# A gated FFT-and-SSM layer with its gradients: a serial copy between the phases is moved, one of two PSUM copies changes engine, PSUM names and table sets are re-planned, and the tail is rebuilt

## The chip, the cores and the metric

The kernel runs on one core of a Trainium2 chip. The metric is the device time of one execution in microseconds (us), less is better. Engines are named as in the profile: PE is TensorE, PEld its weight loads, DVE is VectorE, ACT is ScalarE, POOL is GpSimd, SP is SyncE (used here only to issue DMAs). A name with q (SPq, ACTq) is the engine's instruction queue.

## The reference

```
g  = sigmoid((x * gate_w).sum(-1))                       # x: 2048 x 1024 bf16
a  = irfft2(rfft2(x) * (w_r + i w_i))                    # spectral filter, over both axes
K  = Re sum_n C[d,n] exp(dt[d] A[d,n] l) dt[d] B[d,n]    # S4 kernel, n = 0..127, l = 0..2047
b  = causal_conv(x, K) + x * Dskip                       # by FFT of length 4096
out = g * a + (1 - g) * b
```

The kernel returns `out` (out_0) and, for a given grad_out, the gradients with respect to all twelve inputs: x (out_1), w_r and w_i (out_2, out_3, 2048 x 513 bf16 each), A, B and C real and imaginary (out_4 to out_9, 1024 x 128 bf16 each), log_dt, Dskip and gate_w (out_10 to out_12).

## The kernel before, in words

All Fourier transforms are written as matrix products with tables of sines and cosines. The work has four stages, in this order.

**Phase A**, the two-dimensional spectral filter, is run twice: `run_pass(False)` for the value, `run_pass(True)` for the gradient. The second pass leaves the gradients of w_r and w_i in two DRAM scratch tensors, wgr_scr and wgi_scr, whose rows are padded from 513 to 544 columns. After it stands a barrier over all engines.

**The seam.** The padded rows are copied to out_2 and out_3 through one SBUF tile, wt, of a pool with one buffer: load, store, load, store, all on the GpSimd queue (L569, L570). The pool is closed after that, and the pools of the next stage use its memory: their first loads (PB_c and PB_s, the transform tables, 2 MB each, L592 and L593) wait for it. Some smaller constants follow, and another barrier.

**Phase B**, the state-space convolution, works through eight blocks `bi` of 128 channels. A block loads its columns of x and grad_out (L787, L788), multiplies grad_out by 1 - g (xg_blk, L790), makes tables of powers on ACT and DVE (Exp and Sin, L791 to L831), transforms forward (`FWD`), multiplies the spectra (`CMUL`) and transforms back (`INV`) into GK_blk. Then comes the part that the change touches most, here called the state-space part: 16 sub-blocks of 8 channels, in four groups `tg` of four. For each group:

- `bcast_rows` (L848 to L857) fetches two rows of a small table to SBUF (bc_rows, on the GpSimd queue) and spreads them over 128 partitions by two matmuls into PSUM: into pE and pF for the exponents, into pG and pH for the phases.
- Four pairs of exponentials on ACT make EAg for the whole group (L865, L866).
- Then, for each sub-block: Ts is scaled out of pG and pH on ACT (L874, L875); DVE takes it modulo one turn (FsFc, L880, and again a quarter turn on, L882 and L883); ACT takes the sine twice (L881, L884); DVE multiplies by EAg into AtJ and AtR (L885, L886). In two halves of four channels, TensorE transposes AtJ into pD (L895) and AtR into pC (L898), DVE copies both into the SBUF tile Ad (L900, L901), and TensorE multiplies Ad into psK (L907, L908) and AtJ and AtR into psT (L913). psK and psT lie in pA and pB for even sub-blocks and in pE and pF for odd ones. DVE copies psK out to KT_blk (L914), ACT copies psT out to Tsb (L916).
- After the four sub-blocks, ten DVE operations reduce Tsb to res4 (L923 to L934), which goes to the DRAM scratch res_scr (L936).

Exp and Sin need different function tables on ACT, so a group has two table loads (ACT_TABLE_LOAD, put down to L866 and L881). At the end of the block a last `FWD`, two `CMUL` and an `INV` make this block's output and gradient.

**The tail.** After a last barrier a loop over 16 row tiles adds the gate's part to the gradient of x (gxc, o1c) and multiplies x into gate_w's gradient; the pool fin has two buffers. Then the parameter gradients are loaded, `load_T` transposes the four B and C matrices, `cplx` and single operations compute the rest elementwise on DVE, and, when all six are ready, 48 tiles of 128x128 are transposed, copied (otile) and stored, all on the SP queue.

The order on each engine is that of the program text, moved only by a scheduler that places each instruction by its dependences; semaphores between engines follow from the tiles that an instruction reads and writes.

Of the kernel before, what the change touches and what calls it, by code (L numbers as in the profile page):

```python
# [10 lines left out]
dt = mybir.dt  # L11
ACT = mybir.ActivationFunctionType
ALU = mybir.AluOpType
# [6 lines left out]
def kernel(  # L20
# [10 lines left out]
    nc = tc.nc  # L31
    P = 128
# [5 lines left out]
    SH = S // 2  # L38
# [24 lines left out]

    pid_i = cpool.tile([P, 1], dt.int32, name="pid_i")
# [9 lines left out]
    nc.vector.memset(pio2_b[:], math.pi / 2)  # L74
    zero_b = cpool.tile([P, 1], dt.float32, name="zero_b")
# [124 lines left out]


    if CFG["phaseA"]:
        with ExitStack() as actx:
# [358 lines left out]
            RB = 32  # L562
            NPW = S // RB
            with tc.tile_pool(name="wgout", bufs=1) as wgo:
                for (scr_t, dst) in ((wgr_scr, out_2), (wgi_scr, out_3)):
                    for p0 in range(0, NPW, P):
                        npp = min(P, NPW - p0)
                        wt = wgo.tile([npp, RB, WCOL], dt.bfloat16, name="wt")
                        nc.gpsimd.dma_start(out=wt[:, :, :], in_=scr_t[p0 * RB:(p0 + npp) * RB, 0:WCOL].rearrange("(q r) c -> q r c", r=RB))  # L569
                        nc.gpsimd.dma_start(out=dst[p0 * RB:(p0 + npp) * RB, :].rearrange("(q r) c -> q r c", r=RB), in_=wt[:, :, :])  # L570

    if CFG["phaseB"]:
# [13 lines left out]
        with ExitStack() as bctx:  # L586
# [3 lines left out]
            PB_c = bconst.tile([P, MC, SH + 1], dt.bfloat16, name="PB_c")  # L590
            PB_s = bconst.tile([P, MC, SH + 1], dt.bfloat16, name="PB_s")
# [172 lines left out]
            for bi in range(NBLK):  # L764
# [25 lines left out]
                nc.vector.tensor_tensor(out=xg_blk[:, :, :, DBS:2 * DBS], in0=go_blk[:], in1=omg_bc, op=ALU.mult)  # L790
# [56 lines left out]
                with tc.tile_pool(name="ssm", bufs=1, side="right") as ssmp, tc.tile_pool(name="ssm2", bufs=2, side="right") as ssm2, \  # L847
                        tc.tile_pool(name="bm", bufs=1, side="right") as bm:  # L848
                    def bcast_rows(scr2, dg0, tagA, tagB):
                        rows = ssm2.tile([2, Ds * N], dt.bfloat16, name="bc_rows")  # L850
                        nc.gpsimd.dma_start(out=rows[:, :], in_=scr2[:, dg0:dg0 + Ds, :].rearrange("a d n -> a (d n)"))  # L851
                        HNF = Ds * N // 2
                        ps0 = psB.tile([P, HNF], dt.float32, name=tagA)
                        ps1 = psB.tile([P, HNF], dt.float32, name=tagB)
                        for hh, pst in enumerate((ps0, ps1)):
                            nc.tensor.matmul(pst[:, :], lhsT=ones_row[:, :], rhs=rows[:, hh * HNF:(hh + 1) * HNF], start=True, stop=True)  # L856
                        return ps0, ps1  # L857
                    HNF = Ds * N // 2
                    for tg in range(NTG):
                        Tsb = bm.tile([P, DG, 4, C16], dt.bfloat16, name="Tsb", bufs=2)  # L860
                        EAg = bm.tile([P, TG, Ds * N], dt.bfloat16, name="EAg", bufs=2)
                        for sbl in range(TG):
                            dg0 = d0 + (tg * TG + sbl) * Ds
                            pz0, pz1 = bcast_rows(zr2_scr, dg0, "pE", "pF")
                            nc.scalar.activation(out=EAg[:, sbl, 0:HNF], in_=pz0[:, :], func=ACT.Exp, scale=twop[:, 0:1])  # L865
                            nc.scalar.activation(out=EAg[:, sbl, HNF:2 * HNF], in_=pz1[:, :], func=ACT.Exp, scale=twop[:, 0:1])  # L866
                        for sbl in range(TG):
# [13 lines left out]
                            nc.scalar.activation(out=scv[:, 0, :], in_=FsFc[:, 0, :], func=ACT.Sin, scale=-TWO_PI / (2 ** KFA), bias=pi_b[:])  # L881
                            nc.vector.tensor_single_scalar(out=Ts[:], in_=Ts[:], scalar=(2 ** KFA) // 4, op=ALU.add)  # L882
                            nc.vector.tensor_single_scalar(out=FsFc[:, 1, :], in_=Ts[:], scalar=(2 ** KFA) - 1, op=ALU.bitwise_and)  # L883
                            nc.scalar.activation(out=scv[:, 1, :], in_=FsFc[:, 1, :], func=ACT.Sin, scale=-TWO_PI / (2 ** KFA), bias=pi_b[:])  # L884
                            nc.vector.tensor_tensor(out=AtJ[:], in0=EAg[:, sbl, :], in1=scv[:, 0, :], op=ALU.mult)  # L885
                            nc.vector.tensor_tensor(out=AtR[:], in0=EAg[:, sbl, :], in1=scv[:, 1, :], op=ALU.mult)  # L886
                            psK = psB.tile([P, Ds * C16], dt.float32, name=("pA" if sbl % 2 == 0 else "pE"))
                            psT = psB.tile([P, Ds * 4 * C16], dt.float32, name=("pB" if sbl % 2 == 0 else "pF"))
                            NQ = 4
                            for q in range(Ds // NQ):  # L890
# [10 lines left out]
                                nc.vector.tensor_copy(out=Ad[:, 0, :, :], in_=ptrR[:, :, :])  # L901
# [81 lines left out]

            tc.strict_bb_all_engine_barrier()
            fin = bctx.enter_context(tc.tile_pool(name="fin", bufs=2))
            nc.vector.tensor_reduce(out=gg[:].rearrange("p a b -> p (a b)"), in_=ggall[:].rearrange("p n a b -> p (a b) n"), axis=AX.X, op=ALU.add)
            grad_s = bconst.tile([P, 2, MC], dt.float32, name="grad_s")
# [30 lines left out]
            with tc.tile_pool(name="pg", bufs=1) as pg:  # L1018
                gwr_t = pg.tile([P, D], dt.float32, name="gwr_t")
                gwi_t = pg.tile([P, D], dt.float32, name="gwi_t")  # L1020
                Hr_t = pg.tile([P, D], dt.float32, name="Hr_t")
                Hi_t = pg.tile([P, D], dt.float32, name="Hi_t")
                nc.sync.dma_start(out=gwr_t[:], in_=res_scr[0, :, :])
                nc.sync.dma_start(out=gwi_t[:], in_=res_scr[1, :, :])
                nc.scalar.dma_start(out=Hr_t[:], in_=res_scr[2, :, :])
                nc.scalar.dma_start(out=Hi_t[:], in_=res_scr[3, :, :])
                dt_b = pg.tile([P, D], dt.float32, name="dt_b")
                nc.gpsimd.dma_start(out=dt_b[:], in_=B_log_dt.partition_broadcast(P))
                nc.scalar.activation(out=dt_b[:], in_=dt_b[:], func=ACT.Exp)
                BrT = pg.tile([P, D], dt.bfloat16, name="BrT")  # L1030
                BiT = pg.tile([P, D], dt.bfloat16, name="BiT")
                CrT = pg.tile([P, D], dt.bfloat16, name="CrT")
                CiT = pg.tile([P, D], dt.bfloat16, name="CiT")
                load_T(BrT, B_B_re, 0)
                load_T(BiT, B_B_im, 1)
                load_T(CrT, B_C_re, 0)
                load_T(CiT, B_C_im, 1)
                dBr = pg.tile([P, D], dt.float32, name="dBr2")
                dBi = pg.tile([P, D], dt.float32, name="dBi2")
                nc.vector.tensor_tensor(out=dBr[:], in0=dt_b[:], in1=BrT[:], op=ALU.mult)  # L1040
                nc.vector.tensor_tensor(out=dBi[:], in0=dt_b[:], in1=BiT[:], op=ALU.mult)
                wi_t = pg.tile([P, D], dt.float32, name="wi_t")
                nc.vector.tensor_scalar(out=wi_t[:], in0=wJ[:], scalar1=-1.0, scalar2=None, op0=ALU.mult)
# [10 lines left out]
                gCr = pg.tile([P, D], dt.float32, name="gCr")  # L1054
                gCi = pg.tile([P, D], dt.float32, name="gCi")
                cplx(gCr[:], gCi[:], gwr_t[:], gwi_t[:], dBr[:], dBi[:], True)
                gdBr = pg.tile([P, D], dt.float32, name="gdBr")
                gdBi = pg.tile([P, D], dt.float32, name="gdBi")
                cplx(gdBr[:], gdBi[:], gwr_t[:], gwi_t[:], CrT[:], CiT[:], True)
                gzr = pg.tile([P, D], dt.float32, name="gzr")  # L1060
                gzi = pg.tile([P, D], dt.float32, name="gzi")
                cplx(gzr[:], gzi[:], Hr_t[:], Hi_t[:], wR[:], wi_t[:], True)
                gBr = pg.tile([P, D], dt.float32, name="gBr")
                gBi = pg.tile([P, D], dt.float32, name="gBi")
                nc.vector.tensor_tensor(out=gBr[:], in0=gdBr[:], in1=dt_b[:], op=ALU.mult)
                nc.vector.tensor_tensor(out=gBi[:], in0=gdBi[:], in1=dt_b[:], op=ALU.mult)
                gAr = pg.tile([P, D], dt.float32, name="gAr")
                gAi = pg.tile([P, D], dt.float32, name="gAi")
                nc.vector.tensor_tensor(out=gAr[:], in0=gzr[:], in1=dt_b[:], op=ALU.mult)
                nc.vector.tensor_tensor(out=gAi[:], in0=gzi[:], in1=dt_b[:], op=ALU.mult)  # L1070
                gdp = pg.tile([P, D], dt.float32, name="gdp")
                nc.vector.tensor_tensor(out=gdp[:], in0=gdBr[:], in1=BrT[:], op=ALU.mult)
                nc.vector.tensor_tensor(out=ta[:], in0=gdBi[:], in1=BiT[:], op=ALU.mult)
                nc.vector.tensor_tensor(out=gdp[:], in0=gdp[:], in1=ta[:], op=ALU.add)
                nc.vector.tensor_tensor(out=ta[:], in0=gzr[:], in1=ArT[:], op=ALU.mult)
                nc.vector.tensor_tensor(out=gdp[:], in0=gdp[:], in1=ta[:], op=ALU.add)
                nc.vector.tensor_tensor(out=ta[:], in0=gzi[:], in1=AiT[:], op=ALU.mult)
                nc.vector.tensor_tensor(out=gdp[:], in0=gdp[:], in1=ta[:], op=ALU.add)
                gl = pg.tile([1, D], dt.float32, name="gl")
# [7 lines left out]
                for oi, (src_t, dst) in enumerate(((gAr, out_4), (gAi, out_5), (gBr, out_6), (gBi, out_7), (gCr, out_8), (gCi, out_9))):  # L1087
                    for dc in range(DC):
                        ptq = psB.tile([P, P], dt.float32, name=PSN[(oi * DC + dc) % 4])
                        nc.tensor.transpose(ptq[:, :], src_t[:, dc * P:(dc + 1) * P], ident_f[:, :])  # L1090
                        otile = fin.tile([P, P], dt.bfloat16, name="otile")
# [35 lines left out]
```

## Time and profile before

The median of six runs is 3777.74 us (3773.22 to 3783.92); the profiled execution spans 3775.0 us.

| stage | from, to (us) | length |
|---|---|---|
| phase A | 0 to 882 | 882 |
| seam: copies through wt | 882 to 939 | 57 |
| constants, barrier | 939 to 961 | 22 |
| eight blocks | 961 to 3630 | 2669 |
| of these, the state-space part of block 0 | 1056 to 1212 | 156 |
| tail | 3630 to 3775 | 145 |

In a profile row, `L901 DVE COPY Ad<-pC ... x256 | 108.5, 424 | 87.4 <-PE pC L898 83.2` reads: line 901, a copy on DVE from pC to Ad, 256 times, 108.5 us busy in all and 424 ns each; before them DVE stood idle for 87.4 us, of which 83.2 ended with PE's write of pC at line 898. A row of a table by windows has the stretch, its length, the busy time of PE, PEld, DVE, ACT and POOL with the number of instructions, the granted TensorE clock, the busy share of the DMA engines, and GB/s.

### The profile page before, as it was taken

The numbers are of one execution on the slowest core, as the hardware profiler recorded it, in microseconds if no ns is written. First come the engines' busy times: TensorE is split into PE (matmuls) and PEld (weight loads), VectorE is DVE, ScalarE is ACT, GpSimd is POOL, SyncE is SP. The second block draws the span as 40 slices with busy tenths as digits, with TensorE's granted clock in tenths as the row PEclk, the third lists the DMA queues.
The fourth block names the chain that finished last, engine by engine and source line by source line (L and its number), as shares of the span: only waits on it lengthen the run. The fifth ranks groups of instructions, "written<-read, shape, count | busy, mean of one in ns | idle before, by whom it ended". The sixth has DMA issues, their size and how long they took to land.

```text
span 3775.0 us, 56588 instructions
## 1 busy us (share of the span) xinstructions
PE 2514.2 (67%) x22305; PEld 1594.6 (42%) x22388; DVE 2586.9 (69%) x5624; ACT 1309.9 (35%) x1968; POOL 141.8 (4%) x277
## 2 busy tenths in 40 slices
PE   7789999993566566566656655656665666566553
PEld 3334354441344453444444344434444544454431
DVE  8463129520668868885886888587688868768855
ACT  7211130110354146135514623551462345046300
POOL 0000000000010001000000100000010000001000
PEclk9889999996755775676577568657856865785565
DMA  1320113105200100010010001001000100100051
GB/s 61 110 79 1 53 57 87 30 23 125 76 3 3 34 1 4 14 22 3 4 34 1 4 11 25 3 4 34 1 4 7 30 3 3 35 1 4 4 171 40
DMA packets 201536, 114.15 MB, mean 30 GB/s; under 512 B 164019, under 2 KB 176307, under 8 KB 200886
## 3 DMA queue, kind: packets, MB, share of 16 engines
q1 hardware_dynamic: 106790, 63.26, 5.9%
q10 hardware_dynamic: 83600, 36.22, 3.8%
q0 software_dynamic: 10880, 11.06, 1.6%
q8 instruction: 175, 2.87, 0.3%
q14 instruction: 91, 0.75, 0.1%
HBM read 64.53 MB, written 45.12 MB: 29 GB/s over the span
## 4 chain that ended last, share of the span: by engine, by line
PE 43%; DVE 32%; issue 10%; DMA 9%; ACT 6%; ACTq 0%; SPq 0%; DVEq 0%; POOL 0%; POOLq 0%
PE pC L898 3%; PE pD L895 2%; ACT scv L884 2%; PE pA L760 2%; PE pA L759 2%; PE pE L535 2%; PE pB L760 2%; PE pB L759 1%; PE pE L537 1%; PE pF L913 1%; PE pE L290 1%; DMA go_blk<-in_grad_out_dram 1%; PE pO L290 1%; PE pC L760 1%; PE pC L759 1%
## 5 line engine op out<-in xcount | busy, mean ns | idle before, releaser
L759 PEld LDWEIGHTS <-PB_c 128*128 128x128 bf16 x2048 | 218.2, 109 | 360.0 <-issue 246.0
L895 PE MATMUL pD<-ident,AtJ 128*128 128x128 bf16 x1024 | 153.1, 304 | 233.6 <-DVE AtJ L885 218.8
L759 PE MATMUL pA<-HRt,PB_c 128*128 128x256 bf16 (+1 forms) x512 | 126.7, 302 | 232.7 <-issue 149.0
L760 PEld LDWEIGHTS <-PB_s 128*128 128x128 bf16 x2048 | 223.0, 109 | 27.2 <-issue 1.8
L801 ACT ACT_TABLE_LOAD x32 | 41.1, 1283 | 489.6 <-DMA out_dram<-o0c 468.3
L895 PEld LDWEIGHTS <-AtJ 128*128 128x128 bf16 x1024 | 90.9, 129 | 276.1 <-DVE AtJ L885 258.6
L664 PEld LDWEIGHTS <-PB_c 128*128 128x128 bf16 x1024 | 98.9, 115 | 237.7 <-issue 150.0
L760 PE MATMUL pA<-HJt,PB_s 128*128 128x256 bf16 (+1 forms) x512 | 125.9, 303 | 82.7 <-DVE HJt L752 72.3
L881 ACT ACTIVATE scv<-FsFc,pi_b 128x1024 bf16<-128x1024 int32 x128 | 147.1, 1149 | 91.8 <-DVE FsFc L880 91.4
L884 ACT ACTIVATE scv<-FsFc,pi_b 128x1024 bf16<-128x1024 int32 x128 | 146.5, 1145 | 80.2 <-DVE FsFc L883 80.2
L664 PE MATMUL pA<-xg_blk,PB_c 128*128 128x256 bf16 x256 | 41.9, 319 | 196.1 <-DVE FsB L805 91.9
L901 DVE COPY Ad<-pC 128x512 bf16<-128x512 bf16 x256 | 108.5, 424 | 87.4 <-PE pC L898 83.2
L898 PE MATMUL pC<-ident,AtR 128*128 128x128 bf16 x1024 | 152.8, 304 | 14.9 <-DVE AtR L886 14.3
L913 PEld LDWEIGHTS <-AtJ 128*128 128x128 bf16 x2048 | 158.6, 118 | 0.0
L856 PEld LDWEIGHTS <-ones_row 2*128 2x128 bf16 x512 | 45.1, 100 | 259.6 <-DMA bc_rows<-zr_scr 122.7
L851 POOL DMA_DIRECT2D bc_rows<-zr_scr x128 | 65.4, 512 | 2284.5 <-ACT GK_blk L841 1636.8
L880 DVE TENSOR_SCALAR FsFc<-Ts 128x1024 int32<-128x1024 int32 x128 | 88.3, 690 | 82.6 <-ACT Ts L875 77.4
L913 PEld LDWEIGHTS <-AtR 128*128 128x128 bf16 x2048 | 141.0, 112 | 0.0
L900 DVE COPY Ad<-pD 128x512 bf16<-128x512 bf16 x256 | 107.9, 421 | 38.6 <-PE pD L895 36.1
L856 PE MATMUL pE<-bc_rows,ones_row 2*128 2x512 bf16 x128 | 72.3, 565 | 74.7 <-DMA bc_rows<-zr_scr 43.0
L670 PEld LDWEIGHTS <-PB_s 128*128 128x128 bf16 x1024 | 90.0, 106 | 68.1 <-issue 59.3
L666 PEld LDWEIGHTS <-PB_s 128*128 128x128 bf16 x1024 | 98.2, 114 | 42.6 <-issue 30.7
(531 smaller groups left out, 7525.6 us busy)
## 6 DMA issues: line engine op xcount, KB each, us to landing
Wr_t<-in_A_w_r_dram SPq DMA_DIRECT2D x32, 128.2 KB, 2.5
Wi_t<-in_A_w_i_dram ACTq DMA_DIRECT2D x32, 128.2 KB, 2.6
Yf<-y_scr SPq DMA_DIRECT2D x16, 256.5 KB, 2.8
out_dram<-wt POOLq DMA_DIRECT2D x2, 2052.0 KB, 11.9
a_scr<-och SPq DMA_DIRECT2D x16, 256.0 KB, 2.0
gx_scr<-och SPq DMA_DIRECT2D x16, 256.0 KB, 2.0
ach<-a_scr SPq DMA_DIRECT2D x128, 32.0 KB, 2.0
xga<-gx_scr ACTq DMA_DIRECT2D x128, 32.0 KB, 2.0
```

Source lines behind the costliest of these rows:

```text
L664: nc.tensor.matmul(pER[:, :], lhsT=PB_c[:, mc, ksl], rhs=v[:, 0, mc, :], start=(mc == 0), stop=(mc == MC - 1))
L666: nc.tensor.matmul(pEJ[:, :], lhsT=PB_s[:, mc, ksl], rhs=v[:, 0, mc, :], start=(mc == 0), stop=(mc == MC - 1))
L759: nc.tensor.matmul(pt[:, :], lhsT=PB_c[:, c, nsl], rhs=HRt[:, c, :], start=(i == 0), stop=(i == nmm - 1)); i += 1
L760: nc.tensor.matmul(pt[:, :], lhsT=PB_s[:, c, nsl], rhs=HJt[:, c, :], start=(i == 0), stop=(i == nmm - 1)); i += 1
L856: nc.tensor.matmul(pst[:, :], lhsT=ones_row[:, :], rhs=rows[:, hh * HNF:(hh + 1) * HNF], start=True, stop=True)
L881: nc.scalar.activation(out=scv[:, 0, :], in_=FsFc[:, 0, :], func=ACT.Sin, scale=-TWO_PI / (2 ** KFA), bias=pi_b[:])
L884: nc.scalar.activation(out=scv[:, 1, :], in_=FsFc[:, 1, :], func=ACT.Sin, scale=-TWO_PI / (2 ** KFA), bias=pi_b[:])
L895: nc.tensor.transpose(ptrJ[:, j, :], AtJ[:, dl * N:(dl + 1) * N], ident[:, :])
L898: nc.tensor.transpose(ptrR[:, j, :], AtR[:, dl * N:(dl + 1) * N], ident[:, :])
L900: nc.vector.tensor_copy(out=Ad[:, 1, :, :], in_=ptrJ[:, :, :])
L901: nc.vector.tensor_copy(out=Ad[:, 0, :, :], in_=ptrR[:, :, :])
L913: nc.tensor.matmul(psT[:, tcols], lhsT=lt[:, nsl], rhs=rt, start=True, stop=True)
```

## The change

It has four parts. The copy of the w gradients leaves the seam: in blocks 0 and 1 one DMA each copies a scratch tensor directly from DRAM to its output, ordered behind the block's xg_blk. In the state-space part the copy of pC into Ad goes to ACT, psK and psT always use pA and pB, bc_rows gets buffers of its own for each of the two tables, and ordering constraints without a semaphore (`after_act`) keep Exp and Sin apart on ACT. PB_c and PB_s have a pool of their own, which is released before the tail. In the tail fin gets four buffers, the parameter loads are issued before the loop, elementwise work and stores are interleaved, and otile has six buffers and three queues. A probe option (`extra_kb`) and a constant that nothing reads are added as well.

```diff
             run_pass(True)
             tc.strict_bb_all_engine_barrier()
-            with tc.tile_pool(name="wgout", bufs=1) as wgo:
...
-                        nc.gpsimd.dma_start(out=wt[:, :, :], in_=scr_t[...])
-                        nc.gpsimd.dma_start(out=dst[...], in_=wt[:, :, :])
+            if not CFG["phaseB"]:
+                emit_wgrad_reblock().release()
...
-            PB_c = bconst.tile([P, MC, SH + 1], dt.bfloat16, name="PB_c")
+            pbp = tc.alloc_tile_pool(name="pbp", bufs=1)
+            PB_c = pbp.tile([P, MC, SH + 1], dt.bfloat16, name="PB_c")
...
+                if bi < 2:
+                    rbd = nc.sync.dma_start(out=(out_2, out_3)[bi][:, :], in_=(wgr_scr, wgi_scr)[bi][:, 0:WCOL])
+                    tc.add_manual_dep(rbd.ins, xgm.ins.name, ...Sync..., reason="reblock after the block's loads")
...
-                        rows = ssm2.tile([2, Ds * N], dt.bfloat16, name="bc_rows")
+                        rows = ssm2.tile([2, Ds * N], dt.bfloat16, name="bc_rows_" + tagA, bufs=(2 if tagA == "pE" else 1))
...
+                            if last_sin is not None:
+                                after_act(ex0, last_sin)
+                                after_act(ex1, last_sin)
...
+                            if sbl == 0:
+                                after_act(sn, ex1)
+                                after_act(sn, ex0)
...
-                            psK = psB.tile([P, Ds * C16], dt.float32, name=("pA" if sbl % 2 == 0 else "pE"))
-                            psT = psB.tile([P, Ds * 4 * C16], dt.float32, name=("pB" if sbl % 2 == 0 else "pF"))
+                            psK = psB.tile([P, Ds * C16], dt.float32, name="pA")
+                            psT = psB.tile([P, Ds * 4 * C16], dt.float32, name="pB")
...
-                                nc.vector.tensor_copy(out=Ad[:, 0, :, :], in_=ptrR[:, :, :])
+                                nc.scalar.activation(out=Ad[:, 0, :, :], in_=ptrR[:, :, :], func=ACT.Copy)
...
+            pbp.release()
             tc.strict_bb_all_engine_barrier()
-            fin = bctx.enter_context(tc.tile_pool(name="fin", bufs=2))
+            fin = bctx.enter_context(tc.tile_pool(name="fin", bufs=4))
...
+            load_T(BrT, B_B_re, 0)
...
+            def store_T(src_t, dst, oi):
+                for dc in range(DC):
+                    ptq = psB.tile([P, P], dt.float32, name=PSN[(oi * DC + dc) % 4])
+                    nc.tensor.transpose(ptq[:, :], src_t[:, dc * P:(dc + 1) * P], ident_f[:, :])
+                    otile = fin.tile([P, P], dt.bfloat16, name="otile", bufs=6)
...
+                    (nc.sync, nc.scalar, nc.gpsimd)[(oi * DC + dc) % 3].dma_start(out=dst[dc * P:(dc + 1) * P, :], in_=otile[:])
```

## The prediction

> **What bounds the kernel now.** I read the page first (engine shares, chain of work, costliest groups), then the chain of waits around the seam between the two phases, then one group of the state-space part as a timeline, then a table by windows for the tail.
>
> ```profile
> PE 2514.2 (67%) x22305; PEld 1594.6 (42%) x22388; DVE 2586.9 (69%) x5624; ACT 1309.9 (35%) x1968; POOL 141.8 (4%) x277
> PE 43%; DVE 32%; issue 10%; DMA 9%; ACT 6%; ACTq 0%; SPq 0%; DVEq 0%; POOL 0%; POOLq 0%
> L895 PE MATMUL pD<-ident,AtJ 128*128 128x128 bf16 x1024 | 153.1, 304 | 233.6 <-DVE AtJ L885 218.8
> L901 DVE COPY Ad<-pC 128x512 bf16<-128x512 bf16 x256 | 108.5, 424 | 87.4 <-PE pC L898 83.2
> ```
>
> No engine is full over the span: TensorE and VectorE hand work to each other (the chain is 43% PE, 32% DVE). So gains are read stage by stage. The diff touches three stages.
>
> The seam, from the chain of waits (start, length, what):
>
> ```profile
> 883.33 15.06 issue
> 898.40 11.88 DMA out_dram<-wt
> 910.56 16.26 DMA wt<-wgi_scr
> 927.10 11.88 DMA out_dram<-wt
> 939.12 0.32 SPq L592
> ```
>
> Phase A's last engine work ends near 881.8; then four transfers run one after another on the GpSimd queue while every engine idles, and the load of PB_c (L592) is issued at 939.12.
>
> The state-space part, one turnaround between two groups of four sub-blocks, ACT's timeline (start, length, line, operation, wait before it):
>
> ```profile
> 1118.76 1.15 ACT L881 ACTIVATE scv<-FsFc,pi_b 128x1024 bf16<-128x1024 int32 x1 [1.33 <-DVE FsFc L880]
> 1124.99 0.60 ACT L916 ACTIVATE Tsb<-pF 128x512 bf16<-128x512 f32 x1 [2.71 <-PE pF L913]
> 1125.61 1.28 ACT L866 ACT_TABLE_LOAD   x1
> 1126.90 0.69 ACT L866 ACTIVATE EAg<-pF,twop 128x512 bf16<-128x512 f32 x1
> 1133.93 0.68 ACT L875 ACTIVATE Ts<-pH,twopK 128x512 int32<-128x512 f32 x1
> 1135.81 1.28 ACT L881 ACT_TABLE_LOAD   x1 [1.20 <-DVE res L934]
> 1137.11 1.15 ACT L881 ACTIVATE scv<-FsFc,pi_b 128x1024 bf16<-128x1024 int32 x1
> ```
>
> The first-sine instructions (L881) of this group start at 1101.90, 1105.99, 1111.48, 1118.76, the next group's at 1137.11: steps of 4.1, 5.5, 7.3 and 18.3, in all 35.2 us. The last step is the costly one: the last Tsb copy must leave pF before the next group's exponentials may use pE/pF (L916 before L866), and the ten VectorE operations that follow the group (L923 to L934, 1125.97 to 1135.4) run before the next FsFc, so VectorE and ACT take turns. Busy time in one group:
>
> ```profile
> 1100.60:1135.80 35.20, 23.25 (x273) 14.30 (x272) 28.95 (x51) 23.71 (x30) 4.40 (x9) 0.50 0.03 4
> ```
>
> (PE 23.25, PE weight loads 14.30, DVE 28.95, ACT 23.71.) VectorE is at 82%, ACT at 67%.
>
> The tail, same columns, the last three being granted clock, DMA share and GB/s:
>
> ```profile
> 3630.00:3650.00 20.00, 5.57 (x12) 1.15 (x12) 7.46 (x11) 2.34 (x2) 0.54 (x1) 0.55 0.93 337
> ...
> 3706.00:3737.00 31.00, 7.98 (x18) 2.58 (x18) 27.80 (x29) 1.60 (x6) 0.00 (x0) 0.50 0.05 11
> 3737.00:3775.00 38.00, 15.50 (x34) 6.13 (x34) 6.19 (x21) 5.26 (x19) 0.00 (x0) 0.50 0.15 33
> ```
>
> First loads at 337 GB/s, then VectorE alone, then 48 small stores with every engine mostly idle: three limits one after the other.
>
> **What the Trainium skill says.** "Perfetto Trace Analysis", section "Optimizing Scalar/DVE Operations": where DVE is saturated, moving some operations to Scalar may make sense. The group table agrees that there is room (ACT 67%), though not that ACT is off the path: the timeline shows it in the turnaround. "ScalarE: Activation LUTs", section "What ACT_TABLE_LOAD costs", gives about 1283 ns for the load plus about 1380 ns of drain. The trace shows 1.28 us and the next activation 0.01 us later (1125.61 + 1.28, 1126.90), so I use 1.28. "DMA: Bandwidth & Descriptors", section "Anatomy of one DMA — SWDGE (gpsimd) path", puts some 2.0 us of fixed cost on each transfer; here a 32 KB otile store holds its buffer some 1.5 us, which is why two buffers throttle 48 of them. Its section "Specifications" asks for at least 512 B per transfer element for line rate; the new DRAM-to-DRAM copies have rows of 513 bf16 = 1026 B, so I expect no collapse there; no run so far has such a copy.
>
> **The change, part by part.**
>
> *Seam.* All four transfers go: 939.1 − 881.8 = 57 us of the end-setting chain. In their place two DRAM-to-DRAM copies of 2.1 MB stand on the SP queue, one each in blocks 0 and 1, waiting for the block's xg_blk product (L790, ends near 970). Queued behind that wait on SP is only the next res_scr store, some 140 us later, and nobody before the end reads out_2 or out_3. Bounds for such a copy: 12 us (the store alone) to 28 us (load plus store, as traced); both are shorter than the 86 us of spectrum work before the state-space part's small loads, when the DMA share is a few per cent. Cost nothing. Part: −57 (−50 to −60). PB_c/PB_s in their own pool, the unused options and the new constant cost nothing that a window shows.
>
> *State-space part.* Four edits act together. (a) 256 Ad copies (L901) move from DVE, 0.42 each, to ACT. ACT's price is not traced for this line; a copy of the same shape (L261, xT<-pt_tr, 128x512 bf16) takes 594 ns; the bottom bound is the 0.42 of DVE. I take 0.594, 0.56 from start to start. ACT's busy time per group becomes 23.7 + 8 × 0.594 = 28.5; DVE's 28.95 − 8 × 0.42 = 25.6. (b) psK/psT stay in pA/pB for all sub-blocks, so the next group's exponentials need not wait for pF; but sub-block n+1's 64 psT products must wait for sub-block n's Tsb copy. (c) bc_rows gets three buffers instead of two, so the zr rows are there early. (d) Ordering constraints keep all exponentials of a group between the last sine of one group and the first of the next; table loads stay at one pair per group. In the instruction order of the changed kernel the group's ten VectorE operations now stand interleaved with the next group's FsFc, Ts add and AtJ, and its exponentials among the last sub-block's Ad and Tsb copies.
>
> Putting traced start-to-start durations in that order (sine 1.05, Ad on ACT 0.56, Tsb 0.56, EAg 0.62 to 0.64, Ts 0.57, FsFc/AtJ/AtR 0.60, four transposes 0.40 and 0.2 to drain, 32 psT products 1.0):
> - step within a group: sine 1.05 + Ad 0.56 + second sine 1.17 + wait for it 0.2 + AtR 0.75 + transposes 0.40 + products 1.2 + Tsb 0.56 = 5.9; I get 5.5, 6.6 and 6.1 for the three (before: 4.1, 5.5, 7.3). They lose 1.3 in all.
> - turnaround, ACT back to back: sine 1.05 + Ad 0.56 + sine 1.05 + load 1.28 + EAg 0.64 + wait for pC 0.69 + Ad 0.56 + Tsb 0.56 + seven EAg 4.52 + two Ts 1.15 + DMA issue 0.36 + load 1.28 = 13.7 (before 18.3). It gains 4.6. DVE's ten operations fit in it, ending before the next group's second AtJ.
>
> Group: 18.2 + 13.7 = 31.9 against 35.2. The same arithmetic on the old order gives 35.2, so it can be trusted to some tenths for what it contains. Four groups make a block: 1.2 (the first sine is earlier) + 3 × 3.3 + 0.5 (no turnaround after the last, which still gains from its copies) = 11.6; times 8 blocks = −93 us. With the Ad copy at 0.42 it would be −97. The waits that I can't see (one more semaphore per copy, PE stopping for pB) go one way: −60 to −115.
>
> *Tail.* Loads with four buffers instead of two and the B/C rows fetched at its start: the last transposed row lands 8 us earlier (6 to 10; the first 20 us at 337 GB/s are near what this trace ever shows, so not more). Then 30 elementwise operations of 1.14, 24 casts at 0.2 and the last products make 41 us, with the stores between them on three queues, and 5 us for the last stores: 46 instead of the 69 from 3706 to 3775. Sum −31; I take −28 (−10 to −45).
>
> Total: 57 + 93 + 28 = 178; 3777.7 − 178 = 3600.
>
> **Rivals.**
> - The wait moves: ACT, with 28.5 of 32 us busy, and the single psT buffer give back what the turnaround gains. For it: "ACT Tsb L916 <- PE pF L913" already waits 86 us in all, and within a group my own steps lengthen. Against: the turnaround is 52% of a group and loses a DVE-ACT alternation. Only seam and tail remain: 3777.7 − 85 = 3693.
> - The copies are not hidden (they hold up bc_rows or block loads): seam worth nothing, 3777.7 − 93 − 28 = 3657. Against: the DMA share of 0.03 and nothing queued behind.
> - ACT-bound: the schedule closes every gap, a group takes ACT's 28.5: 6.7 × 32 = −214, and 3777.7 − 57 − 214 − 28 = 3479. Against: the sine-AtR-transpose-Tsb cycle within a sub-block leaves ACT gaps.
> - Slower: psT's buffer serialises the sub-blocks. Unoverlapped, FsFc 0.69, two sines 2.3, AtR 0.69, two rounds of transposes 1.22, two copies 1.2, products 2.4 and Tsb 0.6 make 9.1 a step; three of them and the old turnaround are 45.6, +10.4 × 32 = +333 − 85: 4026; half of that effect gives about 3860. Against: sine and FsFc of n+1 don't touch pB.
>
> **How the numbers follow.** Forecast 0.64, wait moves 0.15, copies not hidden 0.08, ACT-bound 0.07, slower 0.06. The forecast's own bounds reach from 3777.7 − 220 = 3558 to 3777.7 − 120 = 3658. The range 3545 to 3675 adds the copies' case and a little of the partial cases on either side, and leaves out 3693, 3479 and 3860. Faster than 0.2%: 0.94; within: 0.01; slower: 0.05 (the last case, a little of it near zero).
>
> **What would show it.** Right: the spectrum stage starts near 904 instead of 961; L881's starts in a group step by 5.5 to 6.6 and then 13.7; a group window has ACT near 28.5 and DVE near 25.6 busy of 32; the new Ad copy on ACT near 0.59; 118 table loads; the tail near 115 us. Wrong: Tsb or Ad on ACT waiting over 2 us for PE in every sub-block, PE waiting long for Tsb before psT, steps above 7.5, or bc_rows landing much later than 1.8 us in blocks 0 and 1.

## The result, and the profile after

The changed kernel takes 3614.71 us (median of eight runs, 3610.19 to 3617.56) beside 3778.49 us for the kernel before: a ratio of 0.9565, 95% interval 0.9556 to 0.9574. The prediction's point was 3600 us, its range 3545 to 3675. The profiled executions span 3611.9 and 3775.0 us, 163.1 us apart. Split at the first xg_blk product and at the first operation of the tail (gg):

| stretch | before | after | difference | predicted |
|---|---|---|---|---|
| start to the first xg_blk product | 967.45 | 908.26 | -59.2 | -57 |
| eight blocks | 2663.47 | 2588.44 | -75.0 | -93 |
| tail | 144.1 | 115.2 | -28.9 | -28 |

The page of the changed kernel, busy time and the groups that answer to those shown of before:

```profile
PE 2512.9 (70%) x22305; PEld 1587.0 (44%) x22388; DVE 2491.7 (69%) x5369; ACT 1422.4 (39%) x2224; POOL 153.9 (4%) x289
L919 PE MATMUL pD<-ident,AtJ 128*128 128x128 bf16 x1024 | 156.6, 303 | 160.3 <-DVE AtJ L909 116.0
L925 ACT ACTIVATE Ad<-pC 128x512 bf16<-128x512 bf16 x256 | 152.0, 594 | 113.1 <-PE pC L922 110.1
```

The moved copy costs 594 ns on ACT, as the copy of the same shape did; PE's idle time before the transposes fell from 233.6 to 160.3 us. The granted TensorE clock is no rival for the gain: it is 0.96 in phase A in both kernels, and 0.52 before and 0.53 after in the state-space part of block 0.

The seam, as the SP queue's timeline (start, length, line, what is issued):

```profile
880.37 0.32 SPq L603 DMA_DIRECT2D PB_c<-pb_scr  x1
...
901.85 0.38 SPq L798 DMA_DIRECT2D xg_blk<-in_A_x_dram  x1
...
910.58 0.60 SPq L803 DMA_DIRECT2D out_dram<-wgr_scr  x1
```

PB_c is issued at 880.37 instead of 939.12. The issue of the direct copy follows the xg_blk product, and the table of DMA issues has its size and the time to landing:

```profile
out_dram<-wgr_scr SPq DMA_DIRECT2D x1, 2052.0 KB, 24.2
out_dram<-wgi_scr SPq DMA_DIRECT2D x1, 2052.0 KB, 22.9
```

One turnaround between two groups on ACT's timeline:

```profile
1054.11 1.14 ACT L901 ACTIVATE scv<-FsFc,pi_b 128x1024 bf16<-128x1024 int32 x1
...
1056.79 1.28 ACT L882 ACT_TABLE_LOAD   x1
1058.09 0.69 ACT L882 ACTIVATE EAg<-pE,twop 128x512 bf16<-128x512 f32 x1
1058.67 0.59 ACT L925 ACTIVATE Ad<-pC 128x512 bf16<-128x512 bf16 x1
1059.29 0.60 ACT L940 ACTIVATE Tsb<-pB 128x512 bf16<-128x512 f32 x1
...
1066.08 1.28 ACT L901 ACT_TABLE_LOAD   x1
1067.37 1.15 ACT L901 ACTIVATE scv<-FsFc,pi_b 128x1024 bf16<-128x1024 int32 x1
```

The first exponential now runs before the group's last Tsb copy, and nothing stands idle ahead of the second table load. From sine to sine it takes 13.3 us; before it took 18.3. A group by windows (PE, PEld, DVE, ACT, POOL):

```profile
1035.60:1067.40 31.80, 23.70 (x272) 13.90 (x272) 25.91 (x43) 27.23 (x39) 4.20 (x9) 0.50 0.03 5
```

VectorE lost 3 us of busy time in a group, ACT gained 3.5 and is now at 86%. The tail:

```profile
3516.00:3536.00 20.00, 11.70 (x29) 2.47 (x26) 8.66 (x10) 0.83 (x3) 0.00 (x0) 0.55 0.98 334
...
3572.00:3592.00 20.00, 8.91 (x26) 4.40 (x26) 19.93 (x30) 3.75 (x14) 4.30 (x8) 0.50 0.20 48
3592.00:3612.00 20.00, 8.27 (x20) 2.79 (x20) 13.25 (x21) 2.15 (x9) 3.76 (x7) 0.59 0.13 32
```

Stores and elementwise work now share the last 40 us (VectorE 19.93 of 20 busy in the first half), where before 31 us of arithmetic were followed by 38 us of stores.

### The profile page after: what moved, and what is told of

Read it like the earlier page. It is cut to its first block, busy times and chain, and to the rows that moved or that the text cites. A ratio compares the mean times of both kernels' runs of the same rounds, so it can differ in the third digit from the quotient of the medians.

```text
span 3611.9 us, 56654 instructions
## 1 busy us (share of the span) xinstructions
PE 2512.9 (70%) x22305; PEld 1587.0 (44%) x22388; DVE 2491.7 (69%) x5369; ACT 1422.4 (39%) x2224; POOL 153.9 (4%) x289
## 5 line engine op out<-in xcount | busy, mean ns | idle before, releaser
L919 PE MATMUL pD<-ident,AtJ 128*128 128x128 bf16 x1024 | 156.6, 303 | 160.3 <-DVE AtJ L909 116.0
L771 PEld LDWEIGHTS <-PB_s 128*128 128x128 bf16 x2048 | 224.8, 110 | 28.1 <-issue 1.8
L815 ACT ACT_TABLE_LOAD x32 | 41.1, 1283 | 492.0 <-DMA out_dram<-o0c 471.2
L925 ACT ACTIVATE Ad<-pC 128x512 bf16<-128x512 bf16 x256 | 152.0, 594 | 113.1 <-PE pC L922 110.1
L937 PE MATMUL pB<-GK_blk,AtJ 128*128 128x16 bf16 x2048 | 159.6, 194 | 0.0
L909 DVE TENSOR_TENSOR AtJ<-EAg,scv 128x1024 bf16<-128x1024 bf16 x128 | 88.2, 689 | 92.4 <-ACT scv L901 92.4
L865 POOL DMA_DIRECT2D bc_rows_pE<-zr_scr x128 | 68.5, 536 | 1858.0 <-ACT GK_blk L855 1610.1
L931 PE MATMUL pA<-wBR,Ad 128*128 128x16 bf16 x1024 | 90.7, 179 | 80.1 <-ACT Ad L925 80.1
L937 PE MATMUL pB<-GK_blk,AtR 128*128 128x16 bf16 x2048 | 144.3, 194 | 0.0
L931 PEld LDWEIGHTS <-Ad 128*128 128x128 bf16 x1024 | 67.6, 104 | 158.1 <-ACT Ad L925 127.6
```

What stands on the lines that cost most here:

```text
L771: nc.tensor.matmul(pt[:, :], lhsT=PB_s[:, c, nsl], rhs=HJt[:, c, :], start=(i == 0), stop=(i == nmm - 1)); i += 1
L919: nc.tensor.transpose(ptrJ[:, j, :], AtJ[:, dl * N:(dl + 1) * N], ident[:, :])
L925: nc.scalar.activation(out=Ad[:, 0, :, :], in_=ptrR[:, :, :], func=ACT.Copy)
L931: nc.tensor.matmul(psK[:, kcols], lhsT=Ad[:, 0, j, :], rhs=wBR[:, dloc, :], start=True, stop=False)
L937: nc.tensor.matmul(psT[:, tcols], lhsT=lt[:, nsl], rhs=rt, start=True, stop=True)
```

## The experiments

The theory to be tested is the prediction's timetable: each step of the state-space part is a cycle through ACT, VectorE, TensorE and the PSUM names, and no single edit carries the gain. Its expectations for runs that undo or do one edit were worked out from the same durations, put into those kernels' instruction order. Steps are from first sine to first sine, within a group and over the turnaround, medians of the third group unless said otherwise; "blocks" is the stretch from the first xg_blk product to gg, 2588.4 us in the changed kernel. The runs were taken on four chips, on which the kernel before takes 3771.5 to 3780.0 us; each ratio is to the kernel before on the same chip.

### One edit undone: the copy's engine

```diff
-nc.scalar.activation(out=Ad[:, 0, :, :], in_=ptrR[:, :, :], func=ACT.Copy)
+nc.vector.tensor_copy(out=Ad[:, 0, :, :], in_=ptrR[:, :, :])
```

> The changed kernel with the copy of pC into Ad back on VectorE, nothing else. Theory (each step is the cycle through ACT, VectorE and the single psT buffer): the timetable with 0.42 us copies on VectorE gives steps of about 7.7, 7.2, 4.7 and a turnaround of 14.9, a group of 34.5 us instead of 31.8, the state-space part about 9 us longer in each block: +75 us, about 3690. Rival A (the gain is the freed pE/pF and the batching, the copy's engine doesn't matter because VectorE had gaps): within 10 us of 3615. Rival B (VectorE's load alone made the gain): all of the 75 us that the eight blocks gained returns, groups at 35.2 with a turnaround of 18.

Measured: 3664.93 us, ratio 0.9720 (0.9706 to 0.9735) to before, where the changed kernel has 0.9565. Steps 7.75, 7.23, 4.92 and 14.9, as the theory had them; rivals A and B both fall. The blocks grew by 55 us, not 75. The missing 20 us are at the end of a block: from the first sine of a block's last sub-block to the next block's xg_blk product it takes 112.3 us in this run and 114.7 in the changed kernel (means of seven blocks). The trace shows one difference of order there: with the copy on VectorE, a product of 2.3 us (goD, L974) stands behind the block's last reduce (L958), and with the copy on ACT ahead of it; the last reduce ends 23.2 us after that sine here and 24.1 in the changed kernel. Why the other 1.4 us, which lie in the transforms behind it, differ is open. This was the first sign of what the prediction had wrong.

### One edit undone: the PSUM names

```diff
-psK = psB.tile([...], name="pA")
-psT = psB.tile([...], name="pB")
+psK = psB.tile([...], name=("pA" if sbl % 2 == 0 else "pE"))
+psT = psB.tile([...], name=("pB" if sbl % 2 == 0 else "pF"))
```

> The changed kernel with psK and psT alternating between pA/pB and pE/pF again. Theory: the turnaround is the step that pays, because the next group's exponentials wait for pF again: steps of 4.2, 6.3, 6.2 and a turnaround of 16.2 instead of 5.9, 6.6, 6.1 and 13.3, a group of 32.9, about +3 us a block, +23 us in all, about 3638. Rival A (the freed pE/pF carry the gain): +60 us or more, turnaround above 18. Rival C (the single psT buffer costs more inside a group than it gives at the turnaround): faster than the changed kernel by 10 us or more.

Measured: 3638.09 us, ratio 0.9653 (0.9639 to 0.9668), blocks +27 us. Steps 4.2, 6.1, 6.4 and a turnaround of 16.2: the theory's numbers. One buffer instead of two for psK and psT costs 1.8 us inside a group and gives 2.9 at the turnaround (the run doesn't part psK from psT); rivals A and C fall.

### One edit undone: the ordering constraints

```diff
                     def after_act(a, b):
+                        return
```

> The changed kernel without the ordering constraints between exponentials and sines. The scheduler then puts exponentials of the next group between sines of this one: 230 table loads instead of 118 in the instruction order. Theory: each pays 1.28 us on ACT, which has no slack now; steps of about 8.1 and a turnaround of 13.5, +15 us a block, +123 us, about 3737. Rival (table loads hide in ACT's gaps, since ACT is busy only 27 of 32 us): under +30 us.

Measured: 3723.04 us, ratio 0.9875 (0.9858 to 0.9891), blocks +113 us. Steps of the first two groups 7.6 to 8.1 and turnarounds of 13.5; the third group runs 7.6, 8.1 and 6.2 with 6.2 over its turnaround, and the last 12.0, 6.6 and 5.7. The list of groups of this run shows where the loads went (line, count, busy, mean ns, idle before):

```profile
L902 ACT ACT_TABLE_LOAD x88 | 112.9, 1283 | 1.6
L883 ACT ACT_TABLE_LOAD x40 | 51.3, 1283 | 0.7
L884 ACT ACT_TABLE_LOAD x40 | 51.3, 1283 | 0.7
```

168 loads in the state-space part; the changed kernel has 24 + 32 there. The 112 more are 144 us of ACT time, and the blocks grew by 113 us: most of it lies on the path, and the rival falls.

### One edit alone: the PSUM names on the kernel before

The diff is that of the PSUM names above, the other way round, on the kernel before.

> The kernel before with psK and psT in pA and pB for all sub-blocks, nothing else. Theory (freeing pE/pF pays only together with the ordering constraints): exponentials of the next group can now start early and are placed between this group's sines, 246 table loads instead of 118 in the instruction order. Steps of about 8.4, 10.2, 7.5 and a turnaround of 11.8, a group of 37.8 us instead of 35.2, +6.7 us a block: +54 us, about 3832, ratio 1.014. Rival (the shorter turnaround outweighs the loads): faster than before.

Measured: 3839.06 us, slower than before, ratio 1.0162 (1.0145 to 1.0179), blocks +61 us. Steps of the third group 8.3, 10.6, 7.5 and 11.8. Freeing pE and pF does shorten the turnaround, to 11.8, but it also lets a next group's exponential in between two sines, and each costs two table loads. The trace has 246 loads instead of 118, 128 more of 1.28 us each. The edit pays only with the constraints.

### One edit undone: the row buffers

```diff
-name="bc_rows_" + tagA, bufs=(2 if tagA == "pE" else 1)
+name="bc_rows"
```

> The changed kernel with one bc_rows name and two buffers for both tables, as before. Theory: the rows for the first exponentials of a group come later, so the turnaround is 14.5 instead of 13.3 and the first sine of a block about 1.2 us later: +4 us a block, +33 us, about 3648. Rival (small loads are hidden anyway, the other edits carry it): within 8 us of 3615.

Measured: 3633.60 us, ratio 0.9637 (0.9623 to 0.9651), blocks +24 us. The first sine of a block is 1.2 us later (97.9 us after the xg_blk product instead of 96.7) and the turnaround 14.2 us instead of 13.3, nearly as worked out. The steps within a group (6.3, 6.3, 5.7) give a little back, so that the whole is 24 and not 33.

Undone one at a time, the four cost 55 + 27 + 113 + 24 us, together far above the 75 that the blocks gained. They aren't a sum: the edits act on one cycle, and what one is worth depends on the others, as the PSUM names show with and without the constraints.

### The seam put back

```diff
-            if not CFG["phaseB"]:
-                emit_wgrad_reblock().release()
+            emit_wgrad_reblock().release()
...
-                if bi < 2:
+                if False:
```

> The changed kernel with the copies of the w gradients back at the barrier through the tile wt, and without the two copies in blocks 0 and 1. Theory (the removed chain was all exposed and the new copies are hidden): the first xg_blk product comes 59 us later, blocks 0 and 1 keep their 324 us, +59 us, about 3672. Rival (the two new copies, 23 us each, slow the blocks that they run in): less than +59, because blocks 0 and 1 get shorter by several us each.

Measured: 3670.09 us, ratio 0.9725 (0.9708 to 0.9742), 0.0160 or some 60 us above the changed kernel's. The first xg_blk product is at 962.3 us; in the three runs on the same chip that kept the new seam it is at 903.3 to 906.2. The blocks take 2584.4 us without the two copies and, with them, 2588.4 in the changed kernel and 2584.7 to 2588.5 in the three runs on this chip, and blocks 0 and 1 (323.7 and 324.0 us with the copies, 324.3 and 323.4 without) are no longer than the median block (324.1 in both). The copies are hidden; the rival falls.

### The tail, two parts undone

```diff
-name="fin", bufs=4
+name="fin", bufs=2
```

> The changed kernel with two buffers in fin instead of four. Theory (two buffers held back the loads of the tail's first loop): the last transposed row lands some 6 to 9 us later and the tail is 121 to 124 us long instead of 115. Rival (the earlier parameter loads gave the 9 us, the DMA engines are full at 310 to 334 GB/s in the first 40 us either way): tail within 2 us of 115.

Measured: 3617.56 us, ratio 0.9582 (0.9568 to 0.9597); the tail is 120.7 us instead of 115.2, and the last transposed row lands 7.2 us later. The tail varies from run to run: with its code unchanged it took 113.4 and 112.4 us in the two other runs on this chip, and up to 115.7 elsewhere. So the buffers are worth between 5 and 8 us; the ratio, 0.0017 above the changed kernel's, gives some 6. That is about what the theory asked for, and the rival falls.

```diff
-name="otile", bufs=6
+name="otile", bufs=2
...
-(nc.sync, nc.scalar, nc.gpsimd)[(oi * DC + dc) % 3].dma_start(out=dst[...], in_=otile[:])
+nc.sync.dma_start(out=dst[...], in_=otile[:])
```

> The changed kernel with two otile buffers and all its stores on the SP queue, the interleaving kept. Theory (a store holds its buffer 1.5 us, and a VectorE copy that waits for one holds up the elementwise operations behind it on its engine): +10 us, between +6 and +20. Rival (interleaving alone hides the stores): within 2 us of the changed kernel's tail of 115 us.

Measured: 3627.40 us, ratio 0.9606 (0.9590 to 0.9621); the tail is 129.7 us, 14 us or more above the unchanged tail in any other run. The theory holds, above its point of 10 and inside its range: interleaving without free buffers doesn't hide stores.

### The end of a block: where the blocks' missing 18 us are

The changed kernel's waits, and VectorE's timeline at the end of block 0's state-space part:

```profile
ACT fw_t L683 <- DMA res_scr<-res: 156.1, 8, 19.7
```

```profile
1135.14 2.27 DVE L973 TENSOR_TENSOR xDs<-xg_blk,Dskip_b 128x2048 bf16<-128x2048 bf16 x1
...
1137.94 2.27 DVE L974 TENSOR_TENSOR goD<-xg_blk,Dskip_b 128x2048 bf16<-128x2048 bf16 x1
1140.14 1.20 DVE L958 TENSOR_REDUCE res<-p 128x32 f32<-128x1024 bf16 x1
1143.65 0.35 DVE L685 SCALAR_TENSOR_TENSOR fw_or<-pD,ntws,fw_t 128x128 f32<-128x128 f32 x1 [2.30 <-ACT fw_t L683]
```

After a block's last group ACT does nothing for some 20 us until the last res_scr store has landed; then fw_t starts the next transform, and VectorE, which had been busy all along, has stood idle for 2.3 us. In the kernel before the same wait ended as late after the last reduce, but goD ran in it:

```profile
ACT fw_t L672 <- DMA res_scr<-res: 144.8, 8, 18.3
```

```profile
1211.05 1.20 DVE L934 TENSOR_REDUCE res<-p 128x32 f32<-128x1024 bf16 x1
1212.18 2.27 DVE L950 TENSOR_TENSOR goD<-xg_blk,Dskip_b 128x2048 bf16<-128x2048 bf16 x1
1214.58 0.35 DVE L674 SCALAR_TENSOR_TENSOR fw_or<-pD,ntws,fw_t 128x128 f32<-128x128 f32 x1
```

First theory: ACT's own queue, which issues two of those stores.

```diff
-(nc.sync if ri % 2 == 0 else nc.scalar).dma_start(out=res_scr[...], in_=res4[:, ri, :])
+nc.sync.dma_start(out=res_scr[...], in_=res4[:, ri, :])
```

> The changed kernel with all four res_scr stores of a group on the SP queue instead of two of them on ACT's. ACT then isn't held at the end of a block until the last reduce. Theory (the block's end lost what the prediction had given it, because ACT's queue stands at that store and fw_t starts 1.9 us after the last reduce, with the second goD now ahead of it on VectorE): fw_t and fw_or start at least 2 us earlier in each block, -16 us, about 3598, and about 5 us more from the wait that ACT's store has before a group's sines. Rival (VectorE's own order keeps fw_or behind the reduces, and the next block's chain doesn't care): within 4 us of the changed kernel.

Measured: 3610.95 us, ratio 0.9563 (0.9549 to 0.9577), blocks 2588.2. No change. My theory fell, and so did the 5 us that I expected of the sines. With nothing of the store on ACT's queue the wait is still there:

```profile
ACT fw_t L683 <- DMA res_scr<-res: 155.4, 8, 19.7
```

So fw_t waits for the landing itself. It doesn't read res4. The second theory: fw_t is put where res4 was, since the pool of the next stage takes the memory of the pool that ends, and so it must wait until the store has read res4.

```diff
-res4 = bm.tile([P, 4, DG], dt.float32, name="res4")
+res4 = blk.tile([P, 4, DG], dt.float32, name="res4")
```

> The changed kernel with res4 (512 B a partition) in the block's pool instead of the pool bm, nothing else. In the run with the stores on SP, fw_t still waited for the landing of the res_scr store: it isn't ACT's queue, it is memory, because fw_t takes the place in SBUF that res4 leaves. Theory: without that reuse fw_t runs as soon as its products are there, some 15 us earlier, and VectorE goes from the last reduce straight to fw_or instead of standing 2.3 us: -2.3 us in each of the eight blocks, -18 us against the changed kernel, ratio to before about 0.952. Rival (another wait ends at the same place: the landing of something else, or the products): within 4 us of the changed kernel, ratio 0.956 to 0.957.

Measured: 3597.97 us, ratio 0.9524 (0.9511 to 0.9537), blocks -14.4 us. The wait for the landing is gone from the list, and a shorter one has come in its place:

```profile
ACT fw_t L683 <- DVE res L958: 146.5, 8, 18.4
```

```profile
1140.86 1.20 DVE L958 TENSOR_REDUCE res<-p 128x32 f32<-128x1024 bf16 x1
1143.23 0.35 DVE L685 SCALAR_TENSOR_TENSOR fw_or<-pD,ntws,fw_t 128x128 f32<-128x128 f32 x1 [1.17 <-ACT fw_t L683]
```

VectorE's idle time fell from 2.3 to 1.17 us, not to nothing: now it is ACT's queue that holds fw_t, since the second of the two stores on that queue is issued only when the last reduce has ended. In the run before, this hold was hidden behind the later one. That both removed together would close the gap was not tried. The gap explains about 1.2 us of the 1.8 that a block gained. The rest shows in the inverse transform behind it, whose output operations span some 40 or some 42 us in all kernels; five of the eight blocks of this run have the shorter one, and at most one block of any other run. Why is open.

The same edit on the kernel before:

> The kernel before with res4 in the block's pool, nothing else. Theory (before, the second goD of 2.3 us stood behind the last reduce and ran in the shadow of the same wait, so the wait cost nothing; the changed order put goD ahead and bared it): within 4 us of the kernel before. Rival (the wait cost its 2 us a block in the kernel before as well): -16 us, ratio about 0.996.

Measured: 3778.79 us, ratio 0.9999 (0.9991 to 1.0008). The wait for the landing is gone from this run's list too, and the time is the same. The theory holds: there the wait had cost nothing, and it was the changed order that laid it bare.

### A version that beats both

Two of the operations at the end of the state-space part, where VectorE is full, need only x and xg_blk's product, which are there from the start of a block.

```diff
+gpi = nc.vector.tensor_tensor(out=gprod[:], in0=gb_blk, in1=x_blk, op=ALU.mult)
+tc.add_manual_dep(gpi.ins, gkev[0].ins.name, ...Sync..., reason="into the inverse transform")
+nc.vector.tensor_reduce(out=gDacc[:], in_=gprod[:]..., axis=AX.X, op=ALU.add)
...
-nc.vector.tensor_tensor(out=goD[:], in0=gb_blk, in1=x_blk, op=ALU.mult)
-nc.vector.tensor_reduce(out=gDacc[:], in_=goD[:]..., axis=AX.X, op=ALU.add)
```

> As the run with res4 in the block's pool, and the product and reduce for Dskip's gradient (goD 1.2 us, gDacc 3.6 us on VectorE) moved from the end of the state-space part, where VectorE is busy 18.1 of 18.3 us, into the inverse transform ahead of it, where it is busy 4.6 of 24.6 us. Theory: 4.8 us less in each block, -38 us beside the -18, about -56 us against the changed kernel, ratio about 0.942. Rival (VectorE's order puts the reduce before twiddle operations that TensorE needs, and the inverse transform gets as much longer): ratio about that of the run with res4 moved alone.

Measured: 3567.19 us, ratio 0.9437 (0.9424 to 0.9450), blocks 2537.2: 36.8 us less than with res4 moved alone, where 38 were expected; the rival falls. This is the fastest kernel of the study.

## Why the prediction came out

**Seam: right.** -59.2 for -57. The chain was wholly exposed and its replacement wholly hidden. The two direct copies took 24.2 and 22.9 us, and those of the other runs 19.0 to 25.1, inside the bounds of 12 and 28. One reading was a little off: the prediction has engine work of phase A until 881.8, but its last engine operation ends at 879.3 and its last store lands at 881.3; PB_c went out 58.8 us earlier.

**State-space part: the mechanism right, one term mis-sized.** Steps of the second group against the timetable:

| | within a group | turnaround | group |
|---|---|---|---|
| before | 4.1, 5.5, 7.3 | 18.35 | 35.2 |
| predicted | 5.5, 6.6, 6.1 | 13.7 | 31.9 |
| after | 5.87, 6.55, 6.13 | 13.26 | 31.8 |

The first sine came 1.1 us earlier (predicted 1.2), and the three group periods gained 11.0 us in all (9.9). What failed is the term "0.5 (no turnaround after the last, which still gains from its copies)". The working beside it had the three steps of a group lose 1.3 us, and a last group has those steps without the turnaround that pays for them: its steps lost 1.15 us. From the last sub-block's first sine on, another 1.4 us were lost up to the next block, 2.6 in the eighth. Of their mean of 1.6, 0.9 lie ahead of the end of the last reduce, since VectorE's new order runs goD ahead of it (in all four runs with the copy on VectorE goD stands behind it and this stretch takes 23.2 us; in all others but the last version, which has less work there, goD stands ahead and the stretch takes 24.0 to 24.2); the wait behind it stays (2.2 us before, 2.4 after), only that VectorE now idles where goD had filled it; and about half a us lies in the transforms behind, where the cause is open. So a block's end lost 2.6 us where 0.5 had been credited; times eight, that is 25 us, less the 8 us by which the rest was better, and 93 becomes 76. That the miss is 18 and not 25 us is luck: the 8 us are the sum of small errors of the steady steps. The prediction also passed over the wait of fw_t on res_scr in the list of waits: it was in the profile of before, and harmless there.

**Tail: right.** The last transposed row lands 8.4 us earlier (8), and what follows is 20.4 us shorter (23). The prediction's sum was -31, and why it took -28 isn't said; that -28 is so near is in part luck. Removing the buffers of fin gives back 5 to 8 us, and the otile buffers and queues some 15; the earlier parameter loads, the interleaving by itself and the pool of PB_c and PB_s were not separated. The 2.0 us that the prediction cites beside an otile store are the Trainium skill's for transfers issued from GpSimd ("DMA: Bandwidth & Descriptors", "Anatomy of one DMA — SWDGE (gpsimd) path"); the stores of the kernel before stand on SP's queue, and what counts for them is the trace's 1.43 to 1.54 us from issue to landing.

**Rivals.** "The wait moves" took place in small: the single buffers of psK and psT cost 1.8 us a group, measured, and are paid for by the turnaround. "ACT-bound" didn't come: ACT has 27.2 of 31.8 us. "Slower" came only where the PSUM edit was made alone (ratio 1.0162), and there by table loads between the sines and not by the serial sub-blocks that this rival names.

Of the two statements of the Trainium skill that bear on the sum for the state-space part, the first stood: moving some operations from DVE to Scalar paid, 55 us on the chip ("Perfetto Trace Analysis", "Optimizing Scalar/DVE Operations"), although ACT then led the turnaround. Of the second the 1283 ns stood, but of the drain that "ScalarE: Activation LUTs", "What ACT_TABLE_LOAD costs", puts beside them the trace again shows none: the load starts 0.02 us after the sine ahead of it ends, and the exponential 0.02 us after the load.

## What to carry to other kernels

Put the traced durations into the new instruction order, and do it for the last turn of a loop as well as for the steady one: a gain at the turnaround is not there where no turn follows. A wait that costs nothing may be one that other work happens to fill; when an edit moves that work, the wait appears, and its cause can be the memory that a closing pool hands on and not the data or the queue that the instruction names. Edits that free a resource let a scheduler bring work forward, and that needs its own constraint before it pays.

## What the runs showed of the hardware

A DRAM-to-DRAM copy of 2.1 MB in rows of 1026 B took 22.9 and 24.2 us in the changed kernel and 19.0 to 25.1 us in all runs that have it, less than the load (16.3) and the store (11.9) through SBUF together, and the blocks that it ran in were no longer than the others. The run with 112 additional table loads, 144 us of ACT time, took 113 us more in the blocks, although ACT is idle for 14% of a group in the changed kernel: where ACT leads the cycle, its short gaps hid about a fifth of them. A copy of 128x512 bf16 from PSUM took 424 ns on VectorE and 594 ns on ACT.
